# Placement margins for a planned kernel's mixer weights, and another queue for the last ones

## The chip, the cores and the metric

The kernel runs on one core of one Trainium2 chip. Five engines of the core run their own instruction streams: TensorE (PE, with a row PEld for its weight loads), VectorE (DVE), ScalarE (ACT), GpSimd (POOL) and SyncE (SP, which only issues DMA transfers). They are ordered among each other by semaphores alone. The metric is the time of one execution on the device, in microseconds (us), as the median of several runs.

## The reference

Two kinds of layer alternate over a sequence of 2048 rows of width 640, in bf16: A, B, A, B. Layer A is attention with a recurrent memory: the sequence is cut into 64 segments of 32 rows, each is preceded by 8 memory rows that come out of the segment before. Layer B is a mixer: a layer norm, a product with w1, a gelu, shifts along the sequence, a product with w2, then a layer norm and an MLP with w3 and w4.

```
h = concatenate([mem, xs])                  # 8 + 32 rows
q, k, v = h @ Wq, h @ Wk, h @ Wv            # 640 x (32 heads x 192)
p = softmax(where(mask, q k^T * scale, -1e9))
o = (p v) @ Wo                              # (32 x 192) x 640
mem = o[:8]; out = o[8:]

h = gelu(layernorm(x) @ w1); hs = shifted(h) @ w2; x1 = x + hs
B = x1 + gelu(layernorm(x1) @ w3) @ w4

x = x + A(layernorm(x)); x = x + B(layernorm(x))     # twice, with the same weights
```

The memory makes the segments of a layer A run one after the other, and every segment needs all of Wq, Wk, Wv and Wo, some 31 MB, which do not fit on the chip.

## The kernel before

**Steps and lanes.** Both layers A are run together. In step t, lane 0 does segment t of the first layer A and lane 1 does segment t - 5 of the second, side by side in the same matmuls: 2 x 40 = 80 columns (`NS`). There are 69 steps (`T_A`); in the first five and the last five only one lane is at work and the matmuls have 40 columns. In a step the 32 heads go in 8 groups of 4. For each group the matmuls are psk and psq (line 514), psv (line 555), pss (scores, line 586), pst and psvt (transposes), pso (line 634) and psy (the product with Wo, line 653).

**Mixer chunks.** The mixer works on chunks c of 64 rows of each lane, 35 chunks in all (`NCH`). Chunk c is done during steps 2c+2 and 2c+3, its matmuls between those of the attention: psx and psl (transposes of the attention's result, lines 868 and 875), psh with w1 (line 968, 5 weight tiles), hs with w2 (line 994, 5), psh with w3 (line 1025, 10), y with w4 (line 1047, 12). After y, line 1053 on VectorE writes the chunk's result xo, line 1065 on GpSimd stores it, and lines 711 to 731 with line 725 on GpSimd normalize it; psn (line 739) transposes it and three copies on ScalarE (line 1081) put it into hT, the input of lane 1 in the steps that follow. The last chunk's psx waits for line 1053 of the chunk before through the buffer "fin". Chunk 33 runs during step 68, the last; chunk 34 follows alone.

**Weights.** Of the attention's weights a part stays on chip all the time (tiles wk, wq, wv, wo; `CUT`). The rest is streamed in every step, one tile of 128 x 768 or 128 x 640 per transfer, into a ring of 16 slots (tile wst). SyncE issues these transfers (`block`, line 448). The mixer's weights use the same ring; GpSimd issues them (`load_b`, line 472). Class "ra" (attention) may hold at most 14 slots, class "rb" (mixer) at most 5. At most 10 of SyncE's transfers are in flight at a time (`FLIGHT`). For the last two chunks, 33 and 34, the mixer's 32 weight tiles are loaded once, into the resident tiles wk, wq, wv of head groups that step 68 no longer needs (`prefetch`, line 849); both chunks use them from there.

**The order.** No engine's order is written out by hand. Each operation is handed to a planner (`Plan.add`) with an engine, an assumed duration, a due time, and the buffers that it reads and writes. `Plan.place` then walks through a model of the core: it takes, again and again, the engine whose next operation can start first, and among that engine's candidates the one due first; it gives out ring slots and PSUM banks on the way. The result is a fixed order for each engine, and a fixed slot for each load. Transfers have a fixed order per queue, by due time: "wa" for the streamed weights, "wb" for the mixer's. A transfer is modelled as

```
srv = max(s + DMA_LAT, srv) + o.dma / DMA_RATE     # 2.2 us, 345 GB/s
done = srv + DMA_SKEW                              # 2.0 us
```

and what reads it is ready at `done`. The times of the model decide only the order; on the chip every instruction waits for its semaphores. Two lines of `place` matter here: the one that says when a slot counts as free after its last operation (`LAT` = 0.2 us after the end), and the one that says when the readers of a transfer are ready (`at = done`). A due time `base + at * 0.6 * STEP` stands in `prefetch`, with `STEP` = 48 us and `base` the start of step 68.

Of the kernel before, what the change touches and what calls it, by code (L numbers as in the profile page):

```python
# [26 lines left out]
POOL_US = 0.9  # L27
SP_US = 0.47
CUT = {"k": [3] * 8, "q": [3] * 8, "v": [3] * 8, "o": [2] + [4] * 7}
YA = 3  # L30
STEP = 48.0
# [10 lines left out]
LAT = 0.2  # L42
# [3 lines left out]
DMA_LAT = 2.2  # L46
DMA_SKEW = 2.0
FLIGHT = 10


class Buf:
# [34 lines left out]
class Plan:  # L86
# [11 lines left out]
    def add(self, e, d, due, fn, r=(), w=(), a=(), dma=0, queue=None, after=()):  # L98
        op = Op()
        op.e, op.d, op.due, op.fn, op.dma = e, d, due, fn, dma  # L100
        op.succ, op.ready, op.n = [], 0.0, 0
        op.i = len(self.ops)
        preds = set(after)
        slots = []
        for b in r:
            preds.update(b.writers)
        for b in w:
            preds.update(b.writers)
            preds.update(b.readers)
        for b in a:  # L110
            preds.update(b.base)
            preds.update(b.readers)
        for b in r:
            b.readers.append(op)
        for b in w:
            b.base = [op]
            b.writers = [op]
            b.readers = []
        for b in a:
            b.writers.append(op)  # L120
        for b in {id(b): b for b in (*r, *w, *a)}.values():
            if isinstance(b, Slotted):
                b.left += 1
                slots.append(b)
        op.slots = slots
        preds.discard(op)
        for p in preds:
            p.succ.append(op)
            op.n += 1
        self.ops.append(op)  # L130
        if queue is not None:
            self.queues.setdefault(queue, []).append(op)
        return op

    def place(self):
        in_queue = {}
        head = {}
        for q, lst in self.queues.items():
            lst.sort(key=lambda o: (o.due, o.i))
            for k, o in enumerate(lst):  # L140
                in_queue[o.i] = (q, k)
            head[q] = 0
        engines = sorted({o.e for o in self.ops})
        cand = {e: [] for e in engines}
        free = dict.fromkeys(engines, 0.0)
        waiting = {}

        def offer(o):
            if o.i in in_queue:
                q, k = in_queue[o.i]  # L150
                if k != head[q]:
                    waiting[o.i] = o
                    return
            cand[o.e].append(o)

        for o in self.ops:
            if o.n == 0:
                offer(o)
        left = len(self.ops)
        srv = 0.0  # L160
        landed = []
        out = []

        def est(o, t):
            s = max(t, o.ready)
            if o.dma and o.e == "SP" and len(landed) >= FLIGHT:
                s = max(s, landed[-FLIGHT])
            need = {}
            for b in o.slots:
                if b.slot is None:  # L170
                    need[b.cls] = need.get(b.cls, 0) + 1
            for c, n in need.items():
                fs = self.free_slots[self.pool_of[c]]
                al = self.allowed[c]
                if len(fs) < n or len(al) < n:
                    return None
                s = max(s, fs[n - 1][0], al[n - 1])
            return s

        while left:  # L180
            best = None
            for e in engines:
                t = free[e]
                lst = cand[e]
                if not lst:
                    continue
                vals = []
                m = None
                for o in lst:
                    s = est(o, t)  # L190
                    if s is not None:
                        vals.append((s, o))
                        if m is None or s < m:
                            m = s
                if m is None:
                    continue
                if best is not None and m >= best[0]:
                    continue
                lim = m + (LOOK if e == "PE" else 0.05)
                s, o = min((so for so in vals if so[0] <= lim), key=lambda so: (so[1].due, so[1].i))  # L200
                if best is None or s < best[0]:
                    best = (s, o)
            assert best is not None, "no operation can be placed"
            s, o = best
            e = o.e
            for b in o.slots:
                if b.slot is None:
                    b.slot = self.free_slots[self.pool_of[b.cls]].pop(0)[1]
                    self.allowed[b.cls].pop(0)
            o.start = s  # L210
            o.end = s + o.d
            free[e] = o.end
            done = o.end
            if o.dma:
                srv = max(s + DMA_LAT, srv) + o.dma / DMA_RATE
                done = srv + DMA_SKEW
                if e == "SP":
                    landed.append(done)
            cand[e].remove(o)
            out.append(o)  # L220
            left -= 1
            for b in o.slots:
                b.left -= 1
                b.free_at = max(b.free_at, done + LAT)
                if b.left == 0:
                    bisect.insort(self.free_slots[self.pool_of[b.cls]], (b.free_at, b.slot))
                    bisect.insort(self.allowed[b.cls], b.free_at)
            for x in o.succ:
                if o.dma:
                    at = done  # L230
                elif x.e == e:
                    at = o.end
                else:
                    at = o.end + (PE_LAT if e == "PE" else LAT)
                if at > x.ready:
                    x.ready = at
                x.n -= 1
                if x.n == 0:
                    offer(x)
            if o.i in in_queue:  # L240
                q, k = in_queue[o.i]
                head[q] = k + 1
                lst = self.queues[q]
                if k + 1 < len(lst) and lst[k + 1].i in waiting:
                    x = waiting.pop(lst[k + 1].i)
                    cand[x.e].append(x)
        return out
# [3 lines left out]
def kernel(  # L251
# [16 lines left out]
    nc = tc.nc  # L268
    P = 128
# [120 lines left out]
    add = plan.add  # L390
# [63 lines left out]
    def mixer_src(nm, n):  # L454
        if nm == "w1":
            return Dm, B_w1[P * n:P * n + P, :]
        if nm == "w3":
            wd = F // 2
            return wd, B_w3[P * (n % KC):P * (n % KC) + P, wd * (n // KC):wd * (n // KC) + wd]
        if nm == "w4":  # L460
            return Dm, w4_v[:, n, :]
        return Dm, B_w2[P * n:P * n + P, :]
# [375 lines left out]
    def prefetch(c):  # L838

        base = (2 * c + 2) * STEP  # L840
        units = [(nm, n, w[0] + w[1] * n) for nm, k, w in (("w1", KC, W1), ("w2", KC, W2), ("w3", 2 * KC, W3), ("w4", FC, W4))
                 for n in range(k)]
        for i, (nm, n, at) in enumerate(units):
            b, tl = resident["kqv"[i // 3 % 3], i // 9]
            wd, src = mixer_src(nm, n)
            ub = Buf()

            def fn(op, tl=tl, i=i, wd=wd, src=src):
                return nc.gpsimd.dma_start(out=tl[:, i % 3, 0:wd], in_=src)
            add("POOL", POOL_US, base + at * 0.6 * STEP, fn, w=(ub,), a=(b,), dma=P * wd * 2, queue="wb")  # L850
            ahead[nm, n] = ub, lambda tl=tl, i=i, wd=wd: tl[:, i % 3, 0:wd]

    def x2_chunks(a, b):
# [3 lines left out]
    def chunk(c):  # L857
# [99 lines left out]
        if c == NCH - 2:  # L957
            yield
            prefetch(c)
# [173 lines left out]
    for o in placed:  # L1133
        ins = o.fn(o)
        if o.dma and o.e == "SP":
            if len(flight) >= FLIGHT:
                tc.add_manual_dep(ins.ins, flight[-FLIGHT].ins.name,
                                  mybir.DependencyInfo(mybir.DependencyClass.Sync, mybir.DependencyReason.DATA),
# [37 lines left out]
```

## Time and profile before

| what | us |
|---|---|
| median of 7 runs (lowest, highest) | 3527.84 (3517.48, 3535.51) |
| the profiled execution | 3535.51 |
| its span, first to last instruction | 3533.8 |
| PE busy in the span | 3385.0 |
| VectorE, ScalarE, GpSimd busy | 2377.3, 1714.2, 883.8 |
| DMA moved | 1089 MB, 308 GB/s |
| granted TensorE clock | 0.986 |

The profiled execution is the slowest of the seven. The profile shows for each engine the time in which an instruction ran; matmuls overlap each other, so a busy PE is not necessarily a PE at its peak. "Waits" are idle times of an engine, put down to the event that ended them. The "chain" is followed back from the last instruction: at each step to what released it. For transfers the profile has the time from issue to landing, here 4.6 to 4.9 us in the median for the attention's streamed weights and 5.0 and 5.3 us for the mixer's tiles of 160 and 192 KB.

### The profile page before, as it was taken

What the parts mean: (1) busy time and instruction counts of PE and PEld (TensorE: products, weight loads), DVE (VectorE), ACT (ScalarE), POOL (GpSimd) and SP (SyncE); (2) the same over time, 40 slices, a digit from 0 to 9 for tenths busy, and PEclk for the clock granted to TensorE, in tenths of its full rate; (3) what the DMA queues carried; (4) which work ended last, traced back from release to release, by engine and by line L of the source; (5) the groups of instructions that cost most, each with busy time, mean ns of one, the idle gap of its engine ahead of it and who ended that gap; (6) DMA issues with size and microseconds to landing.
All of it is one profiled execution on the core that took longest, in us unless ns stands there. A gap on an engine that the chain in (4) does not pass through costs nothing.

```text
span 3533.8 us, 194661 instructions
## 1 busy us (share of the span) xinstructions
PE 3385.0 (96%) x84693; PEld 3258.6 (92%) x84693; DVE 2377.3 (67%) x7184; ACT 1714.2 (49%) x3583; POOL 883.8 (25%) x1581
## 2 busy tenths in 40 slices
PE   6989999999999999999999999999999999999897
PEld 4879999999999999999999999999999999999786
DVE  2456777777666776776677776776677777766455
ACT  2434555445454555554445554555445545544343
POOL 1022222222222222222222222222222222222222
PEclk9999999999999999999999999999999999999998
DMA  9999999999999999999999999999999999999995
GB/s 341 313 306 306 320 317 316 307 305 314 304 309 309 311 307 307 316 308 312 300 311 318 299 316 313 309 313 311 312 311 311 314 309 311 313 311 310 300 311 195
DMA packets 735258, 1089.24 MB, mean 308 GB/s; under 512 B 95358, under 2 KB 691596, under 8 KB 734400
## 3 DMA queue, kind: packets, MB, share of 16 engines
q1 hardware_dynamic: 669504, 874.19, 75.3%
q0 software_dynamic: 64896, 202.59, 17.1%
q8 instruction: 662, 10.85, 1.3%
q14 instruction: 196, 1.61, 0.1%
HBM read 1071.16 MB, written 5.24 MB: 305 GB/s over the span
## 4 chain that ended last, share of the span: by engine, by line
PE 80%; DMA 14%; issue 4%; DVE 1%; POOL 1%; ACT 0%; SPq 0%; POOLq 0%; DVEq 0%; ACTq 0%
PE psy L653 14%; PE psv L555 14%; PE psq L514 14%; PE psk L514 14%; DMA wst<-in_B_w_dram 5%; PE psvt L567 5%; PE pss L586 4%; PE pso L634 4%; PE psh L1025 3%; DMA wst<-in_A_Wv_dram 3%; DMA wst<-in_A_Wo_dram 2%; PE y L1047 2%; PE pst L619 2%; DMA wst<-in_A_Wq_dram 2%; DMA wst<-in_A_Wk_dram 2%
## 5 line engine op out<-in xcount | busy, mean ns | idle before, releaser
L472 POOL DMA_DIRECT2D wst<-in_B_w_dram x1056 | 581.7, 551 | 1691.7 <-PE psy L653 349.0
L640 DVE CAST oT<-pso 128x480 bf16<-128x480 f32 (+1 forms) x552 | 342.2, 620 | 406.8 <-PE pso L634 405.8
L571 ACT COPY V<-psvt 80x768 bf16<-80x768 bf16 (+1 forms) x552 | 439.3, 796 | 334.2 <-PE psvt L567 325.9
L514 PEld LDWEIGHTS <-wst 128*128 128x128 bf16 x13248 | 555.5, 100 | 34.3 <-issue 9.8
L653 PE MATMUL psy<-oT,wo 128*128 128x80 bf16 (+1 forms) x10350 | 510.7, 199 | 17.5 <-DMA wo<-in_A_Wo_dram 7.9
L522 ACT CAST qT<-psq 128x480 bf16<-128x480 f32 (+1 forms) x552 | 292.5, 530 | 436.8 <-PE psq L514 359.2
L555 PE MATMUL psv<-hT,wv 128*128 128x80 bf16 (+1 forms) x9936 | 478.9, 199 | 7.8 <-issue 4.8
L514 PE MATMUL psk<-hT,wk 128*128 128x80 bf16 (+1 forms) x9936 | 462.8, 199 | 7.7 <-issue 7.0
L514 PE MATMUL psq<-hT,wq 128*128 128x80 bf16 (+1 forms) x9936 | 455.3, 199 | 12.5 <-DMA wq<-in_A_Wq_dram 7.4
L561 ACT CAST vTs<-psv 128x480 bf16<-128x480 f32 (+1 forms) x552 | 292.1, 529 | 338.7 <-PE psv L555 328.7
L653 PEld LDWEIGHTS <-wo 128*128 128x128 bf16 x10350 | 423.4, 100 | 23.8 <-DMA wo<-in_A_Wo_dram 9.1
L597 DVE CUSTOM_DVE_ANT_1 pss<-pss,mask 80x320 f32<-80x320 f32 (+1 forms) x512 | 245.7, 480 | 275.5 <-PE pss L586 234.5
L555 PEld LDWEIGHTS <-wv 128*128 128x128 bf16 x9936 | 405.9, 100 | 21.8 <-issue 5.7
L514 PEld LDWEIGHTS <-wq 128*128 128x128 bf16 x9936 | 394.0, 100 | 21.0 <-DMA wq<-in_A_Wq_dram 8.3
L514 PEld LDWEIGHTS <-wk 128*128 128x128 bf16 x9936 | 398.1, 99 | 15.1 <-issue 7.8
L514 PE MATMUL psk<-hT,wst 128*128 128x80 bf16 (+1 forms) x6624 | 352.8, 199 | 10.9 <-issue 7.2
L653 PE MATMUL psy<-oT,wst 128*128 128x80 bf16 (+1 forms) x6210 | 351.7, 199 | 8.8 <-DMA wst<-in_A_Wo_dram 7.2
L555 PE MATMUL psv<-hT,wst 128*128 128x80 bf16 (+1 forms) x6624 | 342.8, 199 | 10.2 <-DMA wst<-in_A_Wv_dram 8.2
L624 ACT COPY PT<-pst 80x320 bf16<-80x320 bf16 (+1 forms) x552 | 222.9, 404 | 263.4 <-PE pst L619 260.1
L514 PE MATMUL psq<-hT,wst 128*128 128x80 bf16 (+1 forms) x6624 | 327.3, 200 | 7.1 <-DMA wst<-in_A_Wq_dram 4.4
L604 ACT ACTIVATE pss<-pss,sm 80x320 f32<-80x320 f32 (+1 forms) x552 | 261.3, 474 | 137.4 <-DVE sm L597 137.3
L609 DVE TENSOR_REDUCE sm<-pss 80x4 f32<-80x320 f32 (+1 forms) x552 | 251.9, 456 | 93.1 <-ACT pss L604 92.3
(135 smaller groups left out, 5502.1 us busy)
## 6 DMA issues: line engine op xcount, KB each, us to landing
wst<-in_A_Wk_dram SPq DMA_DIRECT2D x1104, 192.0 KB, 4.7
wst<-in_A_Wq_dram SPq DMA_DIRECT2D x1104, 192.0 KB, 4.8
wst<-in_A_Wv_dram SPq DMA_DIRECT2D x1104, 192.0 KB, 4.9
wst<-in_A_Wo_dram SPq DMA_DIRECT2D x1242, 160.0 KB, 4.6
wst<-in_B_w_dram POOLq DMA_DIRECT2D x726, 160.0 KB, 5.0
wst<-in_B_w_dram POOLq DMA_DIRECT2D x330, 192.0 KB, 5.3
wk<-in_A_Wk_dram SPq DMA_DIRECT2D x8, 576.0 KB, 7.3
wq<-in_A_Wq_dram SPq DMA_DIRECT2D x8, 576.0 KB, 7.4
```

Source lines behind the costliest of these rows:

```text
L472: return (nc.sync if B_SP else nc.gpsimd).dma_start(out=T(b)[:, 0:wd], in_=src)
L514: nc.tensor.matmul(out=o[:, c, 0:N], lhsT=w[:, c * P:(c + 1) * P], rhs=h[:, kc, c0:c0 + N], start=pq.begin(), stop=True, skip_group_check= ...
L522: nc.scalar.copy(out=q[:, :, 0:N], in_=T(pq)[:, :, 0:N])
L555: nc.tensor.matmul(out=o[:, c, 0:N], lhsT=w[:, c * P:(c + 1) * P], rhs=h[:, kc, c0:c0 + N], start=pv.begin(), stop=True, skip_group_check= ...
L561: nc.scalar.copy(out=vs[:, :, 0:N], in_=T(pv)[:, :, 0:N])
L571: nc.scalar.copy(out=V_[0:N, :, 0:Dh], in_=T(pt)[0:N].rearrange("n c f -> n (c f)").rearrange("n (i e) -> n i e", i=HG))
L597: nc.vector.tensor_tensor_reduce(out=o, in0=o, in1=maskt.unsqueeze(1).to_broadcast([N, HG, N]), scale=-scale, scalar=3.0e38, op0=ALU.add, ...
L604: nc.scalar.activation(out=o, in_=o, func=ACT.Exp, bias=sm_[0:N, 0:1], scale=-1.0)
L609: nc.vector.reduce_sum(out=sm_[0:N, 4:4 + HG], in_=o, axis=AX.X)
L624: nc.scalar.copy(out=Pt[0:N, :, 0:N], in_=T(pst)[0:N, :, 0:N])
L640: nc.vector.tensor_copy(out=o_[:, :, 0:N], in_=T(pso)[:, :, 0:N])
L653: nc.tensor.matmul(out=T(psy[j])[:, m - m0, c0:c0 + N], lhsT=w[:, m * P:(m + 1) * P], rhs=o_[:, c, 0:N], start=psy[j].begin(), stop=True, ...
```

## The change

Three constants are new, and three places use them. For a transfer that GpSimd issues, the model lets readers start 1.5 us after the modelled landing (`B_SLACK`). A ring slot that a mixer weight held counts as free 0.5 us after its last use instead of 0.2 us (`B_FREE`). And in `prefetch` the 32 transfers of the last two chunks go from GpSimd and queue "wb" to SyncE and queue "wa", due 8 us later than before (`AH`), so that they stand among the streamed weights in order of due time, and take part in the limit of ten transfers in flight. The amount of work, the tiles and the sizes are the same.

```diff
+B_SLACK = 1.5
+AH = 8.0
+B_FREE = 0.5
...
             for b in o.slots:
                 b.left -= 1
-                b.free_at = max(b.free_at, done + LAT)
+                b.free_at = max(b.free_at, done + (B_FREE if b.cls == "rb" else LAT))
...
             for x in o.succ:
                 if o.dma:
-                    at = done
+                    at = done + (B_SLACK if o.e == "POOL" else 0.0)
                 elif x.e == e:
                     at = o.end
...
             def fn(op, tl=tl, i=i, wd=wd, src=src):
-                return nc.gpsimd.dma_start(out=tl[:, i % 3, 0:wd], in_=src)
-            add("POOL", POOL_US, base + at * 0.6 * STEP, fn, w=(ub,), a=(b,), dma=P * wd * 2, queue="wb")
+                return nc.sync.dma_start(out=tl[:, i % 3, 0:wd], in_=src)
+            add("SP", SP_US, base + at * 0.6 * STEP + AH, fn, w=(ub,), a=(b,), dma=P * wd * 2, queue="wa")
             ahead[nm, n] = ub, lambda tl=tl, i=i, wd=wd: tl[:, i % 3, 0:wd]
```

## The prediction, made before the changed kernel ran

> **What bounds the kernel now.** I read the page first (engines, DMA queues, the chain), then busy time by stretch, then PE's waits in the long middle, then one such wait in the chain, and last the order of instructions before and after.
>
> ```profile
> PE 3385.0 (96%) x84693; PEld 3258.6 (92%) x84693; DVE 2377.3 (67%) x7184; ACT 1714.2 (49%) x3583; POOL 883.8 (25%) x1581
> PE 80%; DMA 14%; issue 4%; DVE 1%; POOL 1%; ACT 0%; SPq 0%; POOLq 0%; DVEq 0%; ACTq 0%
> ```
>
> By stretch (us: length; busy and count of PE, weight loads, DVE, ACT, POOL; granted clock; DMA share; GB/s):
>
> ```profile
> 0.00:270.00 270.00, 217.18 (x5440) 188.73 (x5441) 111.84 (x441) 90.76 (x226) 39.35 (x82) 0.94 0.95 319
> 270.00:3200.00 2930.00, 2874.36 (x71837) 2811.45 (x71834) 2079.06 (x6083) 1492.49 (x3040) 756.92 (x1345) 1.00 0.95 311
> 3200.00:3445.00 245.00, 227.12 (x5997) 203.30 (x5995) 136.93 (x491) 102.79 (x248) 61.64 (x110) 0.94 0.94 308
> 3445.00:3504.00 59.00, 52.85 (x1307) 45.40 (x1302) 35.19 (x126) 22.80 (x57) 23.45 (x42) 0.91 0.87 294
> 3504.00:3534.00 30.00, 13.48 (x129) 9.75 (x129) 14.28 (x44) 5.41 (x14) 2.50 (x3) 0.63 0.01 2
> ```
>
> The stretches are: start; the 29 regular chunks of 101 us; the steps with one lane left; the last attention step (68) with chunk 33; chunk 34 alone. In the middle PE is busy 2874 of 2930 us at a granted clock of 1.00, so TensorE sets the pace and only 56 us of idle can be won there. DMA moves 311 GB/s, while the last step reaches 370 to 374 for 15 us on end: bandwidth is near its limit but not at it. So the question is what PE waits for in those 56 us:
>
> ```profile
> PEld L1047 <- issue: 17.0, 28, 1.8
> PE y L1047 <- DMA wst<-in_B_w_dram: 13.7, 25, 1.6
> ...
> PE psy L653 <- DMA wst<-in_A_Wo_dram: 4.6, 6, 1.6
> PE psv L555 <- DMA wst<-in_A_Wv_dram: 2.5, 5, 0.7
> PE psh L1025 <- issue: 2.0, 3, 1.1
> PE psq L514 <- DMA wst<-in_A_Wq_dram: 1.7, 4, 1.1
> PE psk L514 <- DMA wst<-in_A_Wk_dram: 0.4, 1, 0.4
> ```
>
> (us in total, times, longest; the weight load of h2T ahead of y idles for the same cause, so its row and y's are two views of one wait.) The largest single wait is y (w4, line 1047) for a mixer weight. All four kinds of streamed attention weights together make 4.6 + 2.5 + 1.7 + 0.4 = 9.2 us. One case in the chain of waits:
>
> ```profile
> 1722.79 5.64 DMA wst<-in_B_w_dram
> 1728.43 0.04 issue
> 1728.47 0.43 PE y L1047 x2
> ```
>
> POOL issued at 1722.79, as soon as PE had freed the slot; the load landed 5.64 us later and PE stood 0.46 us before y. The placement assumes 2.2 + 2.0 us plus the transfer's share of 345 GB/s, about 4.7 us; the median from issue to landing of these loads is 5.0 (160 KB) and 5.3 us (192 KB). It puts matmuls where a weight lands on time by that model, with nothing to spare.
>
> **The change, part by part.** The two built programs hold the same 84693 matmuls. I counted, for each ring load, the PE work between the last read that frees its slot (or the release of an earlier load in its queue) and its first use, with 36 ns for an 80-column matmul and 136 for a 320-column one (the chain has 18 psv in 0.65 us and 2 y in 0.27).
>
> *1.5 us more for landings on POOL's queue.* In the regular chunk the w1 and w2 matmuls stay put: their leads are 26 us and 9 us already. Of the twelve w4 loads the last seven had leads of 5.7, 6.1, 6.0, 5.3, 5.4, 5.1, 5.2 us of PE work; now 7.1, 7.1, 6.8, 6.5, 6.5, 6.9, 7.6. The longest wait is 1.6 us, the mean 13.7/25 = 0.55, and the leads grow by 0.8 to 2.4 us. So nearly all of it goes; I leave 1 us. Matmul row 13.7, weight-load row 17.0, middle 15.4: **-14 us** (bounds -12.7 and -17). Two tight w3 loads go from 7.2 and 6.7 to 7.8 and 8.2 us, for which the idle is 2.0 + 0.2: **-1.5** (0 to -2.2). The same y wait outside the middle is 14.9 - 13.7 = 1.2 us by the whole-span view: **-1** (0 to -3, as the tight wo and wk loads ahead of step 68 go from 4.4 to 4.9 us to 4.7 to 5.4).
>
> What is late next: while PE stood at y, every load in flight got 0.5 us for nothing. Without that the streamed loads must be in time by themselves. SP's queue has the same order in both programs up to step 68, and the leads of streamed loads barely move: per chunk 14 of 132 are under 6 us before and 10 after, the mean falls by 0.05 to 0.1 of about 8.2 us, for mixer loads now sit longer in the shared ring. Nearest row: those 9.2 us. They can vanish (-9) or double (+9); as a fifth of the y wait coming back seems the nearest, **+3**.
>
> *0.5 instead of 0.2 us until a mixer slot counts as free.* It only moves POOL's loads by up to 1.9 us of PE work (one w3 load from 1603.7 to 1605.4), in w1, w2 and w3 where 9 us or more are spare (the w4 leads above contain it already). Nothing, covered by these leads; without the cover, POOL's next load would be late by as much.
>
> *The last two chunks' 32 loads from POOL to SP.* POOL loses 32 issues of 0.54 us, which nothing waited for but 0.3 us. SP gets 32 of about 0.41 (two in 0.82), 13 us of issue time in a step where it waits for slots. In the built order 20 stand among the streamed loads, and the twelve w4 loads behind the last wo load; queued behind each are the streamed loads, and PE behind those. The 24 w4 matmuls move from among psy to the very end of step 68, in front of chunk 34, whose psx must also wait for line 1053 on their result (0.89 us and some 0.3 of waits; hidden under psy before). From the release of the last wo slot to the last y there are 8.2 us of PE work; the last w4 load needs 12 x 0.41 = 4.9 us of issue and 4.2 to 6.9 to land, so it comes 1 to 3.6 us late. Cost +2 to +5. On the other side step 68 had 59 - 52.85 = 6.1 us of idle and a clock of 0.91, while 32 loads ran in a burst beside the streams (landing of wk and wv 5.5 and 5.6 us there against 4.6 and 4.8) and DMA then fell from 370 to 268, 245 and 141 GB/s. Spread out, most of that idle should go. Net **-3** (bounds +5, nothing won, and -8, idle and some clock won).
>
> A rule that speaks against this part: Trainium Kernel Development and Optimization, Key Constraints, says that the queues of SP, ACT and POOL all run on the same 16 DMA engines, and that issuing from several saves only the sequencer's issue time. By it the move brings no bandwidth and costs 13 us of SP's time; with all of that on the path in place of the -3 the sum would be -0.5. The trace does not show SP alone at its limit, so it cannot settle this.
>
> Sum: -14 - 1.5 - 1 + 3 - 3 = **-16.5 us**. It is made against a profiled execution of 3535.5 us (span 3533.8 and 1.7 around it), which is the slowest of the seven; the median is 3527.84, and 0.2% of it is 7 us, about what a measurement of this kernel tells from no change. I subtract from the median: **3511 us**.
>
> **Rivals.** (1) *The wait moves.* The y idle goes but comes back at psy, psv and psq, as DMA at 311 GB/s has no more to give on time. For: 10 of 132 leads are still under 6 us, and the mean lead shrinks. Against: 370 GB/s in step 68, and an unchanged SP order. With +14 instead of +3 at the streams the time is 3527.84 - 5.5 = 3522 us, or about 3525 if the tail gives nothing. (2) *Slower: the chunk's end comes too late for the next step.* y now ends later, so psn (line 739), its three ACT copies into hT and the reload of xo follow later: psn stands 10.8 us of PE work before the next psx instead of 13.1. In the trace y ends at 1730.5, psn starts at 1735.43, the copies end by 1737.6 at the latest and the next step's first use is at 1747.2, so 9.6 us are spare and 7.3 will be. If ACT's or POOL's queue delays them by more than 7.3 us, each further us costs 29 chunks 29 us: with 1 us over, 3527.84 - 16.5 + 29 = 3540. It decides from 0.8 us over. Against it: POOL's last w1 load waits for a slot only until that same last y, not longer. (3) *More than counted.* The tail wins its 8 us, streams lose 4 us of their wait, and the weight-load row is right: -17 - 2.2 - 3 - 4 - 8 = -34, 3494 us. (4) *The tail loses its 5 us* and the rest holds: 3527.84 - 13.5 + 5 = 3519, still faster.
>
> **How the numbers follow.** Chances: forecast with (4) 0.70, rival (1) 0.15, rival (2) 0.07, rival (3) 0.08. The likeliest case alone spans 3500 to 3520. The range must leave out no more than two tenths: low 3494 at rival (3), high 3526 past rival (1). Faster by over 0.2% (under 3520.8): the forecast, (3) and a small part of (1), 0.80; within 0.2%: most of (1), 0.13; slower: 0.07.
>
> **What would show it.** Right: the row of y waiting for in_B_w in the middle under 3 us; streamed rows together under 13; periods between psx of neighbouring chunks shorter by some 0.5 us; step 68 no longer than its 59 us with no 370 GB/s burst, and y at its end. Wrong: y's idle replaced by psy, psv or psq waiting for DMA (1); PE psk or psx waiting for ACT L1081 or DVE L880 at each step's start (2); psx of chunk 34 later than 58 us after that of chunk 33 (4).

## The result and the profile after

| | before | changed |
|---|---|---|
| median, us (lowest to highest, runs) | 3528.26 (3517.48 to 3556.79, 40) | 3516.05 (3505.99 to 3526.41, 16) |
| ratio, 95% interval | | 0.9964 [0.9952, 0.9976] |
| profiled execution / its span | 3535.51 / 3533.8 | 3515.19 / 3513.5 |

The change makes the kernel 12 us faster (0.36%). The two profiled executions lie 20.3 us apart, since that of before is 7 us above its median; segment sums below are between these two, verdicts between medians.

Busy time by stretch of the changed kernel, the same columns as before (length; PE, weight loads, VectorE, ScalarE, GpSimd; clock; DMA share; GB/s). The bounds are moved so that each stretch holds nearly the same matmuls:

```profile
0.00:270.00 270.00, 217.60 (x5506) 187.71 (x5506) 113.08 (x446) 91.89 (x229) 40.09 (x84) 0.97 0.96 321
270.00:3178.00 2908.00, 2859.96 (x71771) 2802.06 (x71768) 2070.78 (x6077) 1500.59 (x3037) 756.14 (x1343) 1.00 0.95 313
3178.00:3418.00 240.00, 224.16 (x5983) 201.20 (x5981) 136.62 (x491) 102.96 (x247) 60.90 (x110) 0.96 0.95 313
3418.00:3477.00 59.00, 54.60 (x1321) 46.78 (x1318) 34.74 (x125) 22.63 (x57) 5.01 (x9) 0.89 0.92 295
3477.00:3513.00 36.00, 13.63 (x133) 9.73 (x130) 14.99 (x46) 5.41 (x14) 3.01 (x4) 0.72 0.01 4
```

The middle is shorter by 22 us, and DMA moves 313 GB/s in it where it moved 311: the same bytes in less time. The last stretch is 36 us long where it was 30, with the same PE work. That is the surprise of this case, and the profile's waits do not show it.

PE's waits in the middle of the changed kernel (us in total, times, longest):

```profile
PE psv L558 <- DMA wst<-in_A_Wv_dram: 8.9, 18, 1.1
PE psy L656 <- issue: 6.3, 11, 1.4
...
PE psq L517 <- DMA wst<-in_A_Wq_dram: 2.6, 5, 1.3
PE psh L1028 <- issue: 2.5, 4, 1.2
...
PE psy L656 <- DMA wst<-in_A_Wo_dram: 1.0, 3, 0.6
```

(Line numbers are those of before plus 3.) The row of y waiting for a mixer weight, 13.7 us before, is not there any more. The streamed weights have 8.9 + 2.6 + 1.0 = 12.5 us where they had 9.2.

**A balance that closes.** The middle got 22 us shorter, but its idle fell only from 55.6 to 2908 - 2860.0 = 48.0 us. The rest sits inside "busy". The end of a matmul is modelled: one of 80 columns is recorded as 0.20 us long, though the next one starts 0.036 us after it. So the first 0.16 us of a late start leave no idle. I therefore took the time from each matmul's start to the next one's, set the median for each number of columns as its cost (36 ns for 80 columns, 136 for 320), and put what exceeds it by over 60 ns down to the matmul that came late. Both kernels hold the same 71137 matmuls in the 29 regular chunks (2905.6 us before, 2881.8 after):

| late matmul, us | before | changed | difference |
|---|---|---|---|
| y (w4) | 21.4 | 0 | -21.4 |
| psv, psq, psy, psk on streamed tiles | 24.6 | 33.3 | +8.7 |
| psy on the resident wo tiles | 13.1 | 4.3 | -8.8 |
| all the rest | 35.7 | 33.5 | -2.2 |
| sum | 94.8 | 71.1 | -23.7 |

"All the rest" is what remains of the time beyond these costs: some 30 us of other late matmuls in either kernel, and deviations under 60 ns. The 56 us of idle that the prediction took for all that could be won were 95 us by this count, in the 29 chunks.

Outside these chunks: the start -1.0, from psx of chunk 31 to psx of chunk 33 -1.5, step 68 (psx to psx) 57.7 to 57.2, chunk 34 up to its store +0.2, from the store's issue to the end 3.5 to 9.7: +6.2. All together -20.3.

**The end.** The last store, in the timelines of before and of the changed kernel (start, length, what it waited for):

```profile
3530.30 0.58 POOL L1065 DMA_DIRECT2D out_dram<-xo  x1 [11.36 <-DVE xo L1053]
```

```profile
3503.75 0.56 POOL L1068 DMA_DIRECT2D out_dram<-xo  x1 [11.36 <-DVE xo L1056]
```

The spans are 3533.8 and 3513.5. The store lands 1.8 to 1.9 us after its issue in both. What follows in the changed kernel is this, by stretch:

```profile
3504.00:3513.00 9.00, 0.00 (x0) 0.00 (x0) 0.00 (x0) 0.00 (x0) 0.32 (x1) 0.64 0.02 5
```

Nine microseconds with nothing but the end of the store's issue. The raw records name the holder: a DRAIN of GpSimd that begins with the store, 2.76 us long before and 8.99 us in the changed kernel. Neither the busy rows nor the waits count it.

### The profile page after: what moved, and what is told of

It is laid out like the page before. It is cut to its first block, busy times and chain, and to the rows that moved or that the text cites. A ratio compares the mean times of both kernels' runs of the same rounds, so it can differ in the third digit from the quotient of the medians.

```text
span 3513.5 us, 194534 instructions
## 1 busy us (share of the span) xinstructions
PE 3369.9 (96%) x84693; PEld 3247.5 (92%) x84693; DVE 2370.2 (67%) x7184; ACT 1723.5 (49%) x3583; POOL 865.1 (25%) x1549
## 5 line engine op out<-in xcount | busy, mean ns | idle before, releaser
L656 PE MATMUL psy<-oT,wo 128*128 128x80 bf16 (+1 forms) x10350 | 493.3, 199 | 13.7 <-DMA wo<-in_A_Wo_dram 7.8
L558 PE MATMUL psv<-hT,wv 128*128 128x80 bf16 (+1 forms) x9936 | 467.8, 199 | 6.7 <-issue 3.7
L517 PE MATMUL psq<-hT,wq 128*128 128x80 bf16 (+1 forms) x9936 | 458.7, 199 | 12.2 <-DMA wq<-in_A_Wq_dram 7.2
L656 PEld LDWEIGHTS <-wo 128*128 128x128 bf16 x10350 | 412.7, 100 | 18.2 <-DMA wo<-in_A_Wo_dram 8.8
L517 PE MATMUL psq<-hT,wst 128*128 128x80 bf16 (+1 forms) x6624 | 336.9, 199 | 11.1 <-DMA wst<-in_A_Wq_dram 6.7
```

Source lines behind the costliest of these rows:

```text
L517: nc.tensor.matmul(out=o[:, c, 0:N], lhsT=w[:, c * P:(c + 1) * P], rhs=h[:, kc, c0:c0 + N], start=pq.begin(), stop=True, skip_group_check= ...
L558: nc.tensor.matmul(out=o[:, c, 0:N], lhsT=w[:, c * P:(c + 1) * P], rhs=h[:, kc, c0:c0 + N], start=pv.begin(), stop=True, skip_group_check= ...
L656: nc.tensor.matmul(out=T(psy[j])[:, m - m0, c0:c0 + N], lhsT=w[:, m * P:(m + 1) * P], rhs=o_[:, c, 0:N], start=psy[j].begin(), stop=True, ...
```

## The experiments

Twelve kernels, in three groups; each group has runs of before of its own beside it (medians 3529.84, 3531.13, 3526.09). First the numbers of all, from their medians and one profile each. "y", "oT" and "streams" are start-to-start gaps in the 29 chunks, as above; "oT" counts those psy on resident wo that start within 0.15 us of the end of VectorE's oT copy.

| kernel | median (runs) | ratio to before | 29 chunks | y | oT | streams | GpSimd transfers | closing DRAIN |
|---|---|---|---|---|---|---|---|---|
| before | 3528.26 (40) | 1 | 2905.6 | 21.4 | 6.0 | 24.6 | 1314 | 2.76 |
| changed | 3516.05 (16) | 0.9964 [0.9952, 0.9976] | 2881.8 | 0 | 0 | 33.3 | 1282 | 8.99 |
| e1_margins | 3510.93 (7) | 0.9943 [0.9923, 0.9963] | 2874.2 | 1.2 | 0.4 | 24.0 | 1314 | 2.67 |
| e2_slack | 3504.25 (8) | 0.993 [0.9909, 0.995] | 2884.9 | 0.3 | 0 | 29.5 | 1314 | 2.71 |
| e3_move | 3534.99 (12) | 1.0018 [1.0004, 1.0032] | 2899.3 | 16.7 | 6.6 | 22.0 | 1282 | 8.79 |
| e4_free | 3524.4 (12) | 0.9984 [0.9971, 0.9996] | 2892.4 | 14.9 | 6.0 | 24.4 | 1314 | 2.75 |
| e5_after_32 | 3511.0 (6) | 0.9944 [0.9929, 0.9959] | 2880.7 | 0 | 0 | 33.5 | 1314 | 2.78 |
| e6_after_16 | one profile | | 2884.8 | 1.4 | 0 | 41.0 | 1298 | 10.13 |
| e7_slack2 | 3514.2 (8) | 0.9963 [0.9948, 0.9977] | 2879.2 | 0 | 10.5 | 30.9 | 1314 | 2.71 |
| e8_stream1 | 3529.08 (10) | 0.9995 [0.9978, 1.0012] | 2899.5 | 0 | 20.3 | 25.5 | 1314 | 2.71 |
| e9_slack_again | 3505.09 (6) | 0.9934 [0.991, 0.9959] | 2884.1 | 1.0 | 0 | 33.3 | 1314 | 2.72 |
| e10_margins_again | 3508.72 (7) | 0.9948 [0.9929, 0.9968] | 2879.8 | 0.9 | 0.1 | 29.4 | 1314 | 2.71 |
| e11_after_64 | one profile | | 2867.4 | 0 | 0 | 28.1 | 1346 | 5.31 |
| e12_margins_16 | one profile | | 2884.2 | 2.4 | 0.3 | 36.3 | 1330 | 3.19 |

The segment of 29 chunks varies from one execution to the next: e1 and e10 are the same kernel and differ by 5.6 us, before and e3 have the same order there and differ by 6.3, and e2's profile is its slowest run. So single segments are read to some 6 us, the columns "oT" and "DRAIN" to tenths.

### The parts one by one

**e1_margins.** The change without its last part: the 32 loads stay on GpSimd.

```diff
-                return nc.sync.dma_start(out=tl[:, i % 3, 0:wd], in_=src)
-            add("SP", SP_US, base + at * 0.6 * STEP + AH, fn, w=(ub,), a=(b,), dma=P * wd * 2, queue="wa")
+                return nc.gpsimd.dma_start(out=tl[:, i % 3, 0:wd], in_=src)
+            add("POOL", POOL_US, base + at * 0.6 * STEP, fn, w=(ub,), a=(b,), dma=P * wd * 2, queue="wb")
```

> Both margins, the last 32 loads left on GpSimd. Theory A (the longer leads of the w4 loads are the gain): y's wait for a mixer weight in the regular chunks stays under 2 us and the period of a chunk near 99.4 us, as in the changed kernel. Theory B (GpSimd's closing drain, 2.8 us before and 9.0 us after, grows because the loads left GpSimd): the drain is back at 2 to 3 us and the kernel is some 6 us faster than the changed one, about 3510 us, ratio 0.995. If the drain is a matter of chance, the time is that of the changed kernel, 3516, ratio 0.9964. Rival (the move is the gain): ratio 1.000.

**e2_slack.** The same, and the slot margin undone as well.

```diff
-                b.free_at = max(b.free_at, done + (B_FREE if b.cls == "rb" else LAT))
+                b.free_at = max(b.free_at, done + LAT)
```

> Only the 1.5 us for landings. Theory A: all of the gain of the margins, ratio 0.995 to 0.997, y's wait under 2 us. Rival (the later freeing of slots carries a part): ratio 0.998 or more, and y or psh still waits 5 us or more.

**e3_move.** The move alone: the change with both margins at their old values (B_SLACK 0, B_FREE 0.2).

> Only the move of the last 32 loads to SyncE, margins at their old values. Theory A: the regular chunks are those of the kernel before (y waits 11 to 15 us). Tail: step 68 within 1 us of 57.7 us between the two last psx. Theory B: the closing drain is near 9 us and the kernel some 5 us slower than before, ratio 1.001 to 1.002. Rival (the move is the gain): ratio under 0.998.

**e4_free.** The slot margin alone (B_SLACK 0, the loads on GpSimd).

> Only the later freeing of mixer slots (0.5 for 0.2 us). Theory A: leads of w4 loads stay at 5.2 to 6.1 us of TensorE work, so y waits 11 to 15 us as before and the ratio is 1.000 within 0.001. Rival (slots are what counts): ratio under 0.998.

Measured: the landing margin alone makes all of the gain and more, 0.993, and both margins 0.9943. The move alone makes the kernel slower, 1.0018 with an interval above 1. In e3's profile step 68 is 56.6 us, 1.1 less than before. But from psx to psx this step has 57.4 to 59.4 us in the seven profiles with the loads on GpSimd and a margin of 1.5 us or none, and 56.6 to 59.8 in the five with the move, so that a gain there is not shown. The end, from the store's issue on, is 9.8 us, as in the changed kernel, and the closing DRAIN 8.79. Parts and whole fit: -18.9 us (e1) and +5.2 (e3) make -13.7, the change has -12.2.

The waits of e3 in the middle show that without the landing margin y waits as before:

```profile
PE y L1050 <- DMA wst<-in_B_w_dram: 8.1, 16, 1.2
...
PE psv L558 <- DMA wst<-in_A_Wv_dram: 2.6, 5, 0.8
PE psy L656 <- DMA wst<-in_A_Wo_dram: 1.6, 3, 1.1
```

e3's order of the regular chunks is that of before, and e4's w4 leads are (5.2 to 6.1 us). Their y gaps of 16.7 and 14.9 us beside 21.4 tell how far one order varies. e4's 0.9984 may be such variation or a small gain; e9 and e10 below say more.

### Is it the number of GpSimd's transfers?

Two theories for the long DRAIN: it depends on the transfers that GpSimd issued in the whole run, of which the move took 32 away; or on GpSimd having been without transfers in the last steps.

**e5_after_32.** The changed kernel, with 32 transfers of 5 KB by GpSimd added at the start, into a buffer that nobody reads. The last 90 us are as in the changed kernel.

```diff
+    gv = gl[1][:].bitcast(bf16)
+    for i in range(32):
+        def fd(op, i=i):
+            return nc.gpsimd.dma_start(out=gv[:, 20 * i:20 * i + 20], in_=x0d[0:P, 20 * i:20 * i + 20])
+        add("POOL", 0.54, -95, fd, a=(B("gl", 1),), dma=P * 20 * 2)
     start()
```

> The changed kernel with 32 tiny GpSimd transfers (128 rows of 40 bytes, never read) at the very start, so that GpSimd has issued 1314 in all again, as before the change; the last 90 us are those of the changed kernel. Theory C (the closing drain goes by the number of transfers that GpSimd has issued: 1314 gave 2.7 us, 1282 gave 9.0 and 8.8): the drain is 2.7 us again, and the kernel some 6 us faster than the changed one, ratio 0.994 to 0.995. Rival D (it goes by GpSimd having nothing to issue in the last 60 us): the drain stays at 9 us and the ratio at 0.9964.

**e6_after_16.** The same with 16 of them.

> The same with 16 tiny transfers, 1298 in all. Theory C, if the drain falls evenly with the number: 9.0 - 16 x 6.3/32 = 5.9 us. If it depends on a full block of 32 or 64: 9 or 2.7 us. Rival D: 9 us.

e5's last store in its timeline; its span is 3505.2:

```profile
3501.62 0.56 POOL L1068 DMA_DIRECT2D out_dram<-xo  x1 [11.36 <-DVE xo L1056]
```

From the store to the end it is 3.5 us, with a DRAIN of 2.78 us: work added 3.5 ms earlier shortens the end by 6 us. That a GpSimd without late transfers is the cause is refuted, as e5 has none either. e5's ratio, 0.9944, is that of e1 (0.9943): with the DRAIN restored, the move gains nothing that can be measured over the margins alone. The two intervals together leave some 9 us open in either direction, and e5's chunk 2 begins 2 us later than the changed kernel's, behind the added transfers. But e6, half way, did not land half way: 10.13 us. Its one time, 3528.17, is 13 us above the changed kernel's profiled execution; of these the end accounts for 1.1, and a single time is not used here.

**e11_after_64** and **e12_margins_16**, in the last group: 64 such transfers, half as large, added to the changed kernel, and 16 of 5 KB to e1's.

> The changed kernel with 64 tiny GpSimd transfers at the start that nobody reads (1346 in all). If the closing DRAIN is short from some number of GpSimd transfers on (between 1298 and 1314), it is 2.7 us here. If it depends on the number modulo 64 (1282 long, 1298 long, 1314 short), it is about 9 us again, as with 1282.

> Both margins, the 32 loads on GpSimd, and 16 tiny GpSimd transfers at the start that nobody reads (1330 in all). By a threshold between 1298 and 1314 the closing DRAIN is 2.7 us. By the number modulo 64 it is at place 50, which no run has had: no value forecast, but 2.7 would fit a ring whose later half is short, 9 to 10 one with a single short place. If what counts were where the last 90 us issue their transfers and not the number, it is 2.7 us.

The closing DRAIN took 5.31 us in e11 and 3.19 us in e12. Neither a threshold (2.7 for both) nor a period of 64 (about 9 for e11) is right. By number of transfers: 1282 gives 8.8 to 9.0, 1298 10.1, 1314 2.7 to 2.8 (nine profiles), 1330 3.2, 1346 5.3. It rises with the number and falls once between 1298 and 1314. That may be a sawtooth, but five points do not show one; and the transfers added were small ones, so bytes or descriptors may be what counts. The cause inside GpSimd stays open. What is shown is that taking 32 transfers from it put 6.2 us behind the last store, and that 32 others, added at the start, removed these 6.2 us again.

### How much margin, and for whom?

**e7_slack2.** Both margins, loads on GpSimd, with B_SLACK 2.0 instead of 1.5.

> Both margins with 2.0 instead of 1.5 us for landings, last 32 loads on GpSimd. Side effect by the built order: the PE work between the last pso of a chunk's second step and the psy that needs its copy is 0.54 us (0.72 before, where PE stood 0.2 us in every chunk, 6 us in all; 1.08 with 1.5 us, no stall). Theory A': two things made the gain, the leads of the mixer's loads and this gap. So y waits nothing here either, streamed weights wait as with 1.5 us or less, but psy stands 0.38 us in each chunk, 11 us in all: 8 to 12 us slower than e1_margins, ratio 0.997. Theory A alone (only the leads count): 0.994 or better.

**e8_stream1.** Both margins, loads on GpSimd, and 1.0 us more for SyncE's streamed landings too.

```diff
-                    at = done + (B_SLACK if o.e == "POOL" else 0.0)
+                    at = done + (B_SLACK if o.e == "POOL" else 1.0)
```

> Both margins, last 32 loads on GpSimd, and in addition 1.0 us for the landings of SyncE's streamed loads. By the built order only one streamed load per chunk has a lead under 5.4 us of PE work (two in e1), but the gap between the last pso and its psy is 0.18 us. Theory A': streamed weights wait under 5 us in the regular chunks, psy stands 0.74 us per chunk, 21 us in all; net some 13 us slower than e1_margins, ratio near 0.998. Theory A alone: faster than e1_margins by the 8 us of streamed waits, ratio 0.992.

e8's waits in the middle, PE and then its weight loads:

```profile
PE psy L656 <- DVE oT L643: 15.7, 28, 0.6
PE psy L656 <- issue: 9.1, 13, 1.7
...
PE psv L558 <- DMA wst<-in_A_Wv_dram: 1.7, 3, 1.0
PE psq L517 <- DMA wst<-in_A_Wq_dram: 1.5, 2, 1.1
...
PE psy L656 <- DMA wst<-in_A_Wo_dram: 1.2, 2, 0.9
```

```profile
PEld L656 <- issue: 29.3, 42, 1.8
```

By the rows the margin works on what it is given to: the streamed rows are 1.7 + 1.5 + 1.2 and 0.7 for psk, 5.1 us where e1 has 9.1, e10 15.6 and the changed kernel 12.5, and y has none. Start to start it is less clear: the streams have 25.5 us here, 24.0 in e1 and 29.4 in e10. And the time is that of before. The planner has put the last psy of a segment close behind pso: PE stands 28 times, about once a chunk, for VectorE's copy of pso into oT (which takes 0.66 us). In e7 the same row is smaller:

```profile
PE psv L558 <- DMA wst<-in_A_Wv_dram: 7.9, 14, 0.9
PE psy L656 <- DVE oT L643: 5.8, 28, 0.2
```

This explains the -8.8 us at psy in the balance. The built orders hold, between the last pso of a segment and the first psy that needs its copy, this much PE work: before, e3 and e4 0.72 us; the changed kernel, e1 and e2 1.08; e7 0.54; e8 0.18. The oT gaps follow that order without an exception: 6.0 to 6.6 us; 0 to 0.4; 10.5; 20.3. At 0.2 us each they are too short for the profile to list in before (its row "psy <- DVE oT" has one entry of 0.4), and they hide in "busy". So, by the gaps, some 6 us of what the middle gained come from a matmul order that the margin changed by the way. e1 and e7, with margins of 1.5 and 2.0 us, both all but free y; their oT gaps differ by 10 us, and e7 is the slower one (0.9963 against 0.9943, intervals overlapping). But e7's 29 chunks, 2879.2 us in a profile of its fastest run, are no longer than e10's 2879.8, so the 10 us do not show in the segment. No kernel with the old loads and only this gap closed was run either, so its price rests on the gaps in the traces.

### Does the slot margin add anything? And the best version

**e9_slack_again** and **e10_margins_again** are e2 and e1 once more, side by side.

> The landing margin alone, as in e2, once more beside e10 on one chip. If the slot margin is worth nothing, e9 and e10 agree within their intervals (0.993 to 0.994 of before). If the slot margin costs something (e2 3504, e1 3511), e9 stays some 0.0015 below e10; if it gains (e4 at 0.9984), above.

> Both margins, the 32 loads on GpSimd, as in e1. 0.993 to 0.995 of before; closing DRAIN 2.7 us with 1314 GpSimd transfers.

The ratios are 0.9934 and 0.9948, where e2 and e1 had 0.993 and 0.9943. Over both groups the landing margin alone has a median of 3504.2 us (14 runs), both margins 3509.3 (14). The intervals overlap in both groups, so that the slot margin costs something is not shown; that it helps beside the landing margin is not supported either. The landing margin alone, one line, is the best version run here: 0.993 of before, and some 11 us under the changed kernel (3505 against 3516, in different groups).

## Why the prediction was right, and where it was not

The forecast of 3511 us was 5 us below the median, inside its range and on the right side. But the sum is right in part by luck, as its errors cancel. In the two profiles y gave 7 us more than forecast, and the oT copy 6 that no term had; against that the streams took 6 us more, the end took 6 us that no term had, and the gains at w3 and by the move, 4.5 together, came to half a microsecond at most.

- **y (-14 on the middle): right in mechanism, under-sized.** The row went from 13.7 us to nothing. Start to start it was 21.4 us, as the profile's row leaves out what hides in busy; the weight-load row of 17.0 was nearer. e2 has it alone.
- **What is late next (+3): right in sign, under-sized.** By the rows of this pair it is +3.3, but such a row varies by as much: e3, with the order of before in these chunks, has 4.7 us there where before has 9.2. Start to start it is +8.7 in this pair. Over all profiles the streams have 22.0 to 24.6 us without the landing margin (three) and 24.0 to 41.0 with a margin of 1.5 (nine), 23.7 and 32.0 in the mean, so about +8.
- **Not foreseen: the oT copy (-6).** I counted the leads of ring loads only, not what stands between a producer and a consumer on the chip. PE's new order had 0.36 us more work between pso and psy, which is worth 6 us in 29 chunks by the gaps; it made up for the under-sized loss at the streams.
- **w3 (-1.5): not seen.** The idle of psh (line 1025, now 1028) was 2.2 us in the middle and is 2.5, put down to "issue". The longer leads did not shorten it.
- **y outside the middle (-1):** from psx of chunk 31 to psx of chunk 33 it took 1.5 us less, though that is within what single segments vary.
- **The slot margin (nothing):** alone 0.9984, with the landing margin slower if anything. Its leads were unchanged, as counted; the measured effects of up to 5 us of either sign are not explained by them.
- **The move (-3, bounds +5 and -8): wrong, this is the step that failed.** Alone it costs +5.2 us (e3; by its interval +1.4 to +11). The two terms for step 68 held in kind. One of the twelve w4 loads by SyncE came late, and y stood 1.1 us for it; its 24 matmuls, begun at a clock of 0.50, took 5.8 us with 12 short psy among them, where 24 x 0.136 + 12 x 0.025 makes 3.6. Together that is some 3.3 us, within the +2 to +5. Idle of step 68 fell from 6.1 to 59 - 54.6 = 4.4 us, and the burst of 368 to 374 GB/s is gone. The net, -0.5 us in the changed kernel and -1.1 in e3, is not the -3 forecast and lies within what this step varies. What the move cost lay behind the last store, which no term covered.

The highest rates of step 68, in stretches of 5 us, before and in the changed kernel (the last figure is GB/s):

```profile
3460.00:3465.00 5.00, 5.00 (x123) 4.56 (x121) 3.18 (x16) 2.30 (x6) 3.75 (x7) 0.93 1.05 374
```

```profile
3444.00:3449.00 5.00, 3.78 (x109) 3.28 (x107) 2.43 (x11) 2.67 (x6) 0.51 (x1) 0.95 1.03 352
```

The y at the end of the changed kernel, by stretch (the third figure from the end is the clock):

```profile
3464.00:3469.00 5.00, 4.24 (x112) 3.49 (x109) 1.98 (x6) 2.05 (x5) 0.00 (x0) 0.99 0.87 265
3469.00:3474.00 5.00, 3.81 (x41) 2.52 (x41) 0.52 (x3) 0.00 (x0) 0.00 (x0) 0.50 0.86 256
3474.00:3479.00 5.00, 3.20 (x20) 1.96 (x18) 2.06 (x4) 0.00 (x0) 0.60 (x1) 0.82 0.28 94
```

and in its timeline the first y of them, with the wait that began it:

```profile
3470.95 0.69 PE L1050 MATMUL y<-wk,h2T 128*128 128x320 bf16 x2 [1.13 <-DMA wk<-in_B_w_dram]
...
3473.44 1.80 PE L1050 MATMUL y<-wv,h2T 128*128 128x320 bf16 x6
3475.04 1.33 PE L1050 MATMUL y<-wk,h2T 128*128 128x320 bf16 x6
```

**The rivals.** (1) The wait moves: partly true, 8.7 us of 21.4 came back, not 14. (2) psn and hT late: in the middle no row of psk or psx waits for the copies into hT (now line 1084), so it did not happen. (3) More than counted: not in this kernel; e2 comes within some 10 us of its 3494. (4) The tail loses 5 us: the loss is there, its place is not. Its condition, psx of chunk 34 later than 58 us after that of chunk 33, was not met (57.2); the 3519 us that it gave are nearly what was measured.

The rule of the Trainium skill that I had set against the move (Trainium Kernel Development and Optimization, Key Constraints: all issuing queues share the same 16 DMA engines, and several issuers save only issue time) agrees with what the traces show of bandwidth. Over step 68 DMA moved 294 GB/s with the 32 loads on GpSimd and 295 with them on SyncE. The 13 us of SyncE's issue time that I had priced by it do not show on the path, as the step did not get longer (57.7 and 57.2 us). The rule says nothing of the closing DRAIN.

## What to carry to other kernels

Where a planner places readers exactly on the modelled landing, a margin for the late landings is cheap and worth trying alone; give it only to those loads whose waits the profile shows, as a margin for the other queue as well (e8) took the whole gain back elsewhere. When an order changes, compare the gap between every producer and its consumer in the built order, not only the loads: a 0.2 us wait once per chunk left one entry of 0.4 us in the rows, and is 6 us here. And look past the last store: transfers moved away from GpSimd lengthened its closing here, and in the views of the profile only the time from the last issue to the end of the span shows it.

## What the hardware showed that was not expected

- GpSimd's closing DRAIN took 2.7 us with 1314 transfers issued in the run, 8.8 to 9.0 with 1282, 10.1 with 1298, 3.2 with 1330 and 5.3 with 1346, while the last store landed 1.8 to 2.1 us after its issue. Its rule is open.
- TensorE's granted clock fell to 0.50 in the 5 us in which the changed kernel's first late y stood for 1.1 us after two shorter idles, though PE was busy 3.81 us of these 5. The same 0.50 stands in step 68 before the change, from 3455 to 3460 us, with PE busy 4.55 us of 5. What sets it is not shown.
